# Scores of two units made in one run of matmuls, for six pairs of units

## Chip, cores, metric

The kernel runs on one core of one Trainium2 chip. The metric is the device time of one execution in microseconds (us), lower is better. TensorE is called PE below, VectorE DVE, ScalarE ACT, GpSimd POOL, SyncE SP, as the profile does.

## What is computed

```python
for t in range(S):                       # attention with a decaying state, per batch b and head h
    kt, vt, rt = (k[:, :, t], v[:, :, t], r[:, :, t])
    cur = np.einsum('bhd,bhe->bhde', u[None] * kt, vt)
    y[:, :, t] = np.einsum('bhd,bhde->bhe', rt, state + cur)
    state = w[None, :, :, None] * state + np.einsum('bhd,bhe->bhde', kt, vt)
...
h = np.maximum(xt @ w_tok1, 0.0) @ w_tok2        # mixing over the 768 tokens
u = x + h.transpose(0, 2, 1)
h2 = np.maximum(u @ w_ch1, 0.0) @ w_ch2          # MLP over the channels, 384 to 1536 to 384
return (u + h2).astype(np.float32)
```

There are 4 batches, 8 heads, 768 tokens and 48 channels a head; `x` is `y` with its heads side by side, 768 x 384 a batch.

## The kernel before

**Units.** The recurrence is cut into chunks of 128 tokens. One chunk of one batch with all eight heads is a unit: six units a batch, 24 in all, numbered through. The decay is folded into the operands: `kp` and `rp` multiply a unit's k and r by powers of w. PE transposes the two (`trk`, `trr`), and ACT copies them to SBUF as `rk`; for units 14 to 23 a transposing DMA, `t`, which SP issues, does both. Then come the scores, step `at`: for each of four pairs of heads two matmuls of `k` against `r` that contract 48 rows each, one in partitions 0 to 47 and one in partitions 64 to 111, eight in a unit. They write two PSUM banks, one for each half, `at_ps0` and `at_ps1`. Two steps `AT0` and `AT1` on DVE multiply a bank by the causal mask and write bf16; for the halves named in `raw`, ACT copies first and DVE masks the copy. `y` multiplies the masked scores with v, `yS` adds what the state gives, `kv` and `S` advance the state, and `x` adds the diagonal term `yd` and writes the batch's `x_b`.

**The MLP of a batch** follows when its six units are done: `hid` and `hr` (up over the tokens, relu), `bk` and `us` (down, residual), a turn of the result (`tu` and `uT` on PE and ACT or DVE, or a DMA), `z` (up over the channels: 24 steps of 3 matmuls a batch), `zr` (relu, on ACT or DVE), `h` (down: 6 chunks of 4 steps of 3 matmuls) and `os` (residual), then the store. A step `z1_0_9` is batch 1, tokens' half 0, column block 9; `h1_2_3` is batch 1, chunk 2, fourth quarter. The MLP of one batch runs among the units of the next.

**PSUM.** PSUM has eight banks. Four lie in `psA` (L602): one each for `at_ps0`, `at_ps1`, `y_ps` and `kv_ps`. The other four are the pool `psM` (L603), tag `m`: every `trk`, `hid`, `bk`, `tu`, `z` and `h` takes one of these when PE comes to it and gives it back when the last step that reads it is done (`rk`, `hr`, `us`, `uT`, `zr`, `os`). An `h` chunk keeps its bank through all four quarters.

**What sets the order.** `graph` (L181) makes the steps, what each waits for, which take and give a bank. `ORDER` (L508) is a written list for each of the five engines, and the engine works through its list strictly: where a step must wait, all that stands behind it on that engine waits too. `Plan.run` (L70) merges the five lists into one order in which the instructions are recorded; `fill` (L142, L1052) puts small matmuls on idle data, which nothing reads, into waits of PE before the first `z`.

**What the change touches.** The entry for `at` in `graph` (L276 to L303) with the bank lists after it, the configuration `CFG` (L444), all five lists in `ORDER`, and the function `at` (L821).

Of the kernel before, what the change touches and what calls it, by code (L numbers as in the profile page):

```python
# [12 lines left out]
f32 = mybir.dt.float32  # L13
# [8 lines left out]
B, H, S, D = 4, 8, 768, 48  # L22
T = 128
C = S // T
G = C // 2
HP = H // 2
# [154 lines left out]
def graph(do, cfg):  # L181
# [48 lines left out]
    kus, rkus, adgs, raws, masked = [], [], [], [], []  # L230
    for u in range(NU):
# [44 lines left out]
        at = p.add(f"at{u}", [("PE", t_at * f, t_at * f + 0.2)], [rk, rkk] + at_free, rank=r, emit=do("at", u))  # L276
# [7 lines left out]
        if u in cfg.get("raw2", ()):  # L284
            raw0 = p.add(f"raw0_{u}", [("ACT", 0.5, 0.65)], [atq[0]] + raws[-1:] + masked[-3:][:len(masked) // 3 and 1], rank=r, emit=do("raw", u, 0))
            a0 = p.add(f"AT0_{u}", [("DVE", 0.33, 0.48, True)], [raw0], rank=r, emit=do("ATr", u, 0))
            raws.append(raw0)
            masked.append(a0)
        else:
            raw0 = a0 = p.add(f"AT0_{u}", [("DVE", 0.597, 0.75)], [atq[0]], rank=r, emit=do("AT", u, 0))  # L290
        if u in cfg.get("raw", ()):
            raw = p.add(f"raw{u}", [("ACT", 0.5, 0.65)], [at] + raws[-1:] + masked[-3:][:len(masked) // 3 and 1], rank=r, emit=do("raw", u, 1))
# [3 lines left out]
            at_free = [raw0, raw]  # L296
        else:
            a1 = p.add(f"AT1_{u}", [("DVE", 0.597, 0.75)], [atq[1]], rank=r, emit=do("AT", u, 1))
            at_free = [raw0, a1]
# [138 lines left out]
    for s in p.steps:  # L438
# [60 lines left out]
    y_m=(2, 4),  # L499
    apart=2.0,  # L500
# [70 lines left out]
def kernel(  # L571
# [477 lines left out]
    def do(kind, *args):  # L1049
        return lambda eng: STEPS[kind](eng, *args)  # L1050
# [52 lines left out]
```

## Time and profile before

| | us |
|---|---|
| time, median of 3 executions | 165.9 (165.4 to 166.22) |
| the profiled execution, its own time | 164.99 |
| its span, first to last instruction | 163.2 |

The span and what lies around it differ by 1.79 us. In the profile, almost every instruction carries line L617, since one helper records them all; so groups are told apart by the names of what they write and read: `z_ps` is written by `z`, `h_ps` by `h` and also by `hid` (then it reads `x_b`), `hT_ps` by `bk`, `t_ps` by `tu`, `tr_ps` by `trk` and `trr`, `at_ps` by `at` (and, in three steps ahead of the first `z`, by the turn of batch 0), `kv_ps<-UW,pr` by `pg`, a small product for the diagonal term. A row of a timeline gives the start, the time to the end of the last instruction in the row, and how many instructions it holds. The end of a matmul is modelled and overlaps the next one, so what a matmul costs PE is read from start to start.

### The profile page before, as it was taken

The numbers are of one execution on the slowest core, as the hardware profiler recorded it, in microseconds if no ns is written. First come the engines' busy times: TensorE is split into PE (matmuls) and PEld (weight loads), VectorE is DVE, ScalarE is ACT, GpSimd is POOL, SyncE is SP. The second block draws the span as 40 slices with busy tenths as digits, with TensorE's granted clock in tenths as the row PEclk, the third lists the DMA queues.
The fourth block names the chain that finished last, engine by engine and source line by source line (L and its number), as shares of the span: only waits on it lengthen the run. The fifth ranks groups of instructions, "written<-read, shape, count | busy, mean of one in ns | idle before, by whom it ended". The sixth has DMA issues, their size and how long they took to land.

```text
span 163.2 us, 3866 instructions
## 1 busy us (share of the span) xinstructions
PE 154.2 (95%) x1510; PEld 99.8 (61%) x1510; DVE 115.9 (71%) x245; ACT 73.6 (45%) x158; POOL 69.1 (42%) x85
## 2 busy tenths in 40 slices
PE   6977999999999999899999999999999999999991
PEld 3555876666666667576566665665666666665571
DVE  5369996826397999795969979898989574222621
ACT  4898683362579633656623540082226102731200
POOL 7449860000363977998439201887527100000000
PEclk9999999999999999999999999999999999999999
DMA  5999999999998999889969989999971036100412
GB/s 107 219 218 221 167 185 205 185 184 202 204 220 167 234 237 196 156 143 210 190 153 214 207 203 179 191 220 171 228 184 51 0 72 156 65 0 0 145 54 96
DMA packets 97428, 26.28 MB, mean 161 GB/s; under 512 B 90753, under 2 KB 97410, under 8 KB 97410
## 3 DMA queue, kind: packets, MB, share of 16 engines
q1 hardware_dynamic: 93920, 22.88, 69.0%
q0 software_dynamic: 3488, 3.15, 12.3%
q8 instruction: 12, 0.20, 0.5%
q14 instruction: 6, 0.05, 0.1%
q10 hardware_dynamic: 2, 0.00, 0.0%
HBM read 20.65 MB, written 4.72 MB: 155 GB/s over the span
## 4 chain that ended last, share of the span: by engine, by line
PE 86%; ACT 5%; DVE 5%; issue 2%
PE h_ps L617 33%; PE z_ps L617 27%; PE y_ps L617 5%; PE at_ps L617 5%; PE hT_ps L617 4%; PE tr_ps L617 4%; ACT rk L617 3%; PE kv_ps L617 3%; PE idle_ps L617 2%; DVE AT L617 2%; PE w_ps L617 1%; PE t_ps L617 1%; PE fill_ps L617 1%; DVE pr L617 1%; DVE x_b L617 1%
## 5 line engine op out<-in xcount | busy, mean ns | idle before, releaser
L617 PE MATMUL h_ps<-wch,zr 128*128 128x384 bf16 (+1 forms) x300 | 55.2, 320 | 0.0
L617 ACT ACTIVATE zr<-z_ps 128x384 bf16<-128x384 f32 x66 | 31.1, 492 | 50.0 <-PE z_ps L617 49.8
L617 PE MATMUL z_ps<-uT,wch 128*128 128x384 bf16 x288 | 53.2, 326 | 0.0
L617 PEld LDWEIGHTS <-wch 128*128 128x128 bf16 x288 | 26.9, 98 | 16.2
L617 PEld LDWEIGHTS <-zr 128*128 128x128 bf16 x300 | 27.4, 98 | 14.9
L617 DVE TENSOR_TENSOR AT<-at_ps,mask 128x512 bf16<-128x512 f32 x43 | 28.8, 683 | 1.7 <-PE at_ps L617 1.6
L617 POOL TENSOR_TENSOR kpr<-ld_k,wn 128x384 bf16<-128x384 f32 x18 | 17.8, 996 | 22.2 <-DMA ld_k<-in_k_dram 20.5
L617 DVE TENSOR_SCALAR zr<-z_ps 128x384 bf16<-128x384 f32 x30 | 16.1, 552 | 11.8 <-PE z_ps L617 11.8
L617 POOL TENSOR_TENSOR yd<-vb,adg 128x384 f32<-128x384 bf16 x15 | 12.6, 840 | 21.3 <-DVE adg L617 14.9
L617 ACT COPY rk<-tr_ps 128x512 bf16<-128x512 bf16 (+1 forms) x23 | 15.3, 682 | 12.3 <-PE tr_ps L617 12.2
L617 DVE TENSOR_TENSOR osb<-u_sb,h_ps 128x384 f32<-128x384 bf16 (+1 forms) x22 | 11.7, 533 | 12.0 <-PE h_ps L617 11.8
L617 POOL TENSOR_TENSOR kpr<-ld_r,wp 128x384 bf16<-128x384 f32 x16 | 16.9, 1059 | 7.9 <-DVE x_b L617 2.5
L617 PEld LDWEIGHTS <-kpr 128*128 128x128 bf16 x192 | 12.4, 99 | 6.8 <-issue 2.6
L617 PEld LDWEIGHTS <-rk 48*128 48x128 bf16 (+1 forms) x272 | 10.6, 95 | 7.6 <-issue 3.9
L617 ACT CAST vb<-ld_v 128x384 bf16<-128x384 f32 x24 | 12.1, 513 | 4.1 <-DMA ld_v<-in_v_dram 4.0
L617 DVE TENSOR_TENSOR x_b<-y_ps,yd 128x384 bf16<-128x384 f32 x23 | 12.7, 552 | 0.7 <-PE y_ps L617 0.4
L617 DVE TENSOR_TENSOR u_sb<-x_b,hT_ps 128x384 bf16<-128x384 bf16 x21 | 10.8, 550 | 3.1 <-PE hT_ps L617 3.0
L617 PE MATMUL tr_ps<-ident,kpr 128*128 128x128 bf16 x112 | 10.6, 227 | 2.1 <-ACT rk L617 1.4
L617 PEld LDWEIGHTS <-wtok 128*128 128x128 bf16 x90 | 8.2, 97 | 4.5
L617 PE MATMUL h_ps<-x_b,wtok 128*128 128x384 bf16 x48 | 10.1, 326 | 0.0
L617 PE MATMUL at_ps<-rk 48*128 48x128 bf16 x192 | 9.5, 219 | 0.5 <-ACT rk L617 0.4
L617 POOL TENSOR_TENSOR ku<-ld_k,u_bc 128x384 f32<-128x384 f32 x9 | 8.9, 994 | 0.6 <-DVE kpr L617 0.6
(87 smaller groups left out, 156.4 us busy)
## 6 DMA issues: line engine op xcount, KB each, us to landing
ld_r<-in_r_dram SPq DMA_DIRECT2D x24, 192.0 KB, 3.8
ld_k<-in_k_dram SPq DMA_DIRECT2D x24, 192.0 KB, 3.8
ld_v<-in_v_dram SPq DMA_DIRECT2D x24, 192.0 KB, 3.9
out_dram<-osb SPq DMA_DIRECT2D x23, 192.0 KB, 3.0
wch<-in_moe_w_ch_dram POOLq DMA_DIRECT2D x4, 576.0 KB, 11.8
wtok<-in_moe_w_tok_dram POOLq DMA_DIRECT2D x2, 384.0 KB, 6.3
u_bc<-in_u_dram SPq DMA_DIRECT2D x1, 192.0 KB, 5.4
out_dram<-osb SPq DMA_DIRECT2D x2, 96.0 KB, 1.6
```

Source lines behind the costliest of these rows:

```text
L617: ins = tc.keep_in_program_order(f(*args, **kw))
```

## The change

In six pairs of units (6 and 7, 12 and 13, 14 and 15, 16 and 17, 18 and 19, 22 and 23) the step `at` of the second unit goes, and the first one's makes the scores of both: sixteen matmuls in a row. The first unit's scores go to `at_ps0` and `at_ps1` of `psA` as before. The second unit's go to two banks of `psM`, which two new steps without instructions (`at14_bank0`, `at14_bank1`) reserve; each is given back when the step that reads it (`AT`, or `raw` where ACT copies) is done. The run now waits for the transposed operands of both units.

```diff
+        pairs, give = cfg.get("pairs", ()), [[], []]
+        if u - 1 in pairs:
+            for s in [at] + at_bank:
+                p.wait(s, [rk, rkk])
+            give = [[f"at{u - 1}_bank{q}"] for q in range(2)]
+        elif u in pairs:
+            at_bank = [p.add(f"at{u}_bank{q}", [("PE", 0.0, 0.0)], [rk, rkk] + at_free, take=True, rank=r) for q in range(2)]
+            at = p.add(f"at{u}", [("PE", t_at + 0.14, t_at + 0.29)], [rk, rkk] + at_bank + at_free, rank=r, emit=do("at", u, True))
+        else:
+            at = p.add(f"at{u}", [("PE", t_at * f, t_at * f + 0.2)], [rk, rkk] + at_free, rank=r, emit=do("at", u))
...
-            at_free = [raw0, a1]
+            free = [raw0, a1]
+        if u - 1 not in pairs:
+            at_free = free
...
+    pairs=(6, 12, 14, 16, 18, 22),
...
-    def at(eng, i):
+    def at(eng, i, both=False):
...
+        if both:
+            L[i + 1]["at"] = [psM.tile([128, HP, T], f32, name=f"at_ps{q}", tag="m") for q in range(2)]
+        for n in range(i, i + 1 + both):
+            L[n]["AT"] = [None, None]
+            for a in range(HP):
+                for q in range(2):
+                    half = slice(q * P, q * P + D)
+                    pe.matmul(L[n]["at"][q][:, a, :], L[n]["rk"][half, 0, a, :], L[n]["rk"][half, 1, a, :],
+                              start=True, stop=True)
```

All five lists of `ORDER` are written anew as well, from the first step to the last. PE's step list holds the same work but for the pairs; eight more `zr`, one more `uT` and one more `os` stand on DVE instead of ACT, five `adg` more on ACT instead of DVE; SP issues the same 112 transfers in another order; PE's program has 44 fill matmuls instead of 50. Its list around units 14 and 15, a line of each:

```diff
-        "z1_0_0 z1_0_5 z1_0_9 z1_0_8 tu1_5 z1_0_1 tu1_4 z1_0_6 z1_0_11 z1_1_0 at14 z1_0_10 z1_1_3 z1_0_4 z1_0_2 z1_0_7 y13 z1_0_3 at15 "
+        "z1_1_6 z1_1_3 z1_0_3 z1_1_1 y13 z1_1_2 kv14 z1_0_6 z1_0_11 h1_1_0 yS14 at14_bank0 h1_1_1 at14_bank1 at14 h1_0_0 h1_0_1 h1_1_2 "
```

Three places show what moved. First PE, at the last matmuls of unit 14's scores. Before, `rk_1471` is unit 14's operand, `at_ps0_1587` and `at_ps1_1588` its two banks, and the `z` of the MLP follows at once:

```order
L617 LDWEIGHTS rk_1471
L617 MATMUL at_ps0_1587<-rk_1471 128x128
L617 LDWEIGHTS rk_1471
L617 MATMUL at_ps1_1588<-rk_1471 128x128
L617 LDWEIGHTS wch1_154
L617 MATMUL z_ps_1600<-uT_1264,wch1_154 128x384
```

Now unit 14's last two (`rk_1583`) are followed by the first of unit 15 (`rk_1522`), which write two banks of `psM`, `at_ps0_1682` and `at_ps1_1683`:

```order
L629 LDWEIGHTS rk_1583
L629 MATMUL at_ps0_1680<-rk_1583 128x128
L629 LDWEIGHTS rk_1583
L629 MATMUL at_ps1_1681<-rk_1583 128x128
L629 LDWEIGHTS rk_1522
L629 MATMUL at_ps0_1682<-rk_1522 128x128
L629 LDWEIGHTS rk_1522
L629 MATMUL at_ps1_1683<-rk_1522 128x128
```

Between the two units' scores there is no other matmul now, where six `z` and one `y` stood between `at14` and `at15` before. Behind the run stand `h1_0_0 h1_0_1 h1_1_2 h1_1_3 z1_1_9 kv15 y14`.

Second, DVE at the masks of these two units. Before, unit 14's two `AT` stand together, and unit 15's come with other work between:

```order
L617 TENSOR_TENSOR AT1_1616<-at_ps1_1588,mask_114 128x512
L617 TENSOR_TENSOR AT0_1622<-at_ps0_1587,mask_114 128x512
L617 TENSOR_TENSOR S0_1631<-kv_ps_1329,bm_137 128x384
L617 TENSOR_SCALAR zr_1510<-z_ps_1612 128x384
L617 TENSOR_TENSOR x_b2_158<-y_ps_1465,yd_1578 128x384
L617 TENSOR_REDUCE adg_1665<-rku_1533 128x8
L617 TENSOR_TENSOR AT1_1677<-at_ps1_1648,mask_114 128x512
```

Now all four stand within six rows, and unit 15's first bank is read ahead of unit 14's second:

```order
L629 TENSOR_TENSOR AT0_1704<-at_ps0_1680,mask_114 128x512
L629 TENSOR_TENSOR AT0_1713<-at_ps0_1682,mask_114 128x512
L629 TENSOR_REDUCE adg_1613<-rku_1458 128x8
L629 TENSOR_TENSOR AT1_1727<-at_ps1_1681,mask_114 128x512
L629 TENSOR_SCALAR zr_1586<-z_ps_1632 128x384
L629 TENSOR_TENSOR AT1_1759<-at_ps1_1683,mask_114 128x512
```

Third, DVE at the start of the program, where no pair stands. Before, unit 0 goes ahead: `kp0`, `rp0`, then `kp1` (`kpr0_123` holds unit 0's products, `kpr1_125` unit 1's):

```order
L617 TENSOR_TENSOR kpr0_123<-ld_k_162,wn_146 128x8x48
L617 TENSOR_TENSOR kpr0_123<-ld_r_160,wp_147 128x8x48
L617 TENSOR_TENSOR kpr1_125<-ld_k_168,wn_146 128x8x48
L617 TENSOR_TENSOR AT0_230<-at_ps0_210,mask_114 128x512
L617 TENSOR_TENSOR pr_240<-tr_ps_185,rk_198 128x512
```

Now unit 1's k product stands between unit 0's two, and the diagonal's `pr` ahead of the mask:

```order
L629 TENSOR_TENSOR kpr0_123<-ld_k_162,wn_146 128x8x48
L629 TENSOR_TENSOR kpr1_125<-ld_k_160,wn_146 128x8x48
L629 TENSOR_TENSOR kpr0_123<-ld_r_164,wp_147 128x8x48
L629 COPY wu_sb_148<-wu_ps_211 128x4
L629 TENSOR_TENSOR UW_133<-wu_sb_148,wu_ps_211 64x4 x2
L629 TENSOR_TENSOR pr_244<-tr_ps_188,rk_202 128x512
L629 TENSOR_TENSOR AT0_251<-at_ps0_234,mask_114 128x512
```

Unit 0's r product moved one place back, and on ACT the table for unit 1's k (`wn1`) now stands ahead of unit 0's (`wn0`).

More of the change, by code (lines that the diff above doesn't have):

```diff
@@ L284, in graph @@
         if u in cfg.get("raw2", ()):
-            raw0 = p.add(f"raw0_{u}", [("ACT", 0.5, 0.65)], [atq[0]] + raws[-1:] + masked[-3:][:len(masked) // 3 and 1], rank=r, emit=do("raw", u, 0))
+            raw0 = p.add(f"raw0_{u}", [("ACT", 0.5, 0.65)], [atq[0]] + raws[-1:] + masked[-3:][:len(masked) // 3 and 1], rank=r, give=give[0], emit=do("raw", u, 0))
             a0 = p.add(f"AT0_{u}", [("DVE", 0.33, 0.48, True)], [raw0], rank=r, emit=do("ATr", u, 0))
@@ L289, in graph @@
         else:
-            raw0 = a0 = p.add(f"AT0_{u}", [("DVE", 0.597, 0.75)], [atq[0]], rank=r, emit=do("AT", u, 0))
+            raw0 = a0 = p.add(f"AT0_{u}", [("DVE", 0.597, 0.75)], [atq[0]], rank=r, give=give[0], emit=do("AT", u, 0))
         if u in cfg.get("raw", ()):
-            raw = p.add(f"raw{u}", [("ACT", 0.5, 0.65)], [at] + raws[-1:] + masked[-3:][:len(masked) // 3 and 1], rank=r, emit=do("raw", u, 1))
+            raw = p.add(f"raw{u}", [("ACT", 0.5, 0.65)], [at] + raws[-1:] + masked[-3:][:len(masked) // 3 and 1], rank=r, give=give[1], emit=do("raw", u, 1))
             a1 = p.add(f"AT1_{u}", [("DVE", 0.33, 0.48, True)], [raw], rank=r, emit=do("ATr", u, 1))
@@ L295, in graph @@
             masked.append(a1)
-            at_free = [raw0, raw]
+            free = [raw0, raw]
         else:
-            a1 = p.add(f"AT1_{u}", [("DVE", 0.597, 0.75)], [atq[1]], rank=r, emit=do("AT", u, 1))
-            at_free = [raw0, a1]
+            a1 = p.add(f"AT1_{u}", [("DVE", 0.597, 0.75)], [atq[1]], rank=r, give=give[1], emit=do("AT", u, 1))
+            free = [raw0, a1]
+        if u - 1 not in pairs:
+            at_free = free
         if cfg.get("at_one"):
@@ L826, in at @@
             L[i]["at"] = [psA.tile([128, HP, T], f32, name=f"at_ps{q}", tag=f"at{q}") for q in range(2)]
-        L[i]["AT"] = [None, None]
-        for a in range(HP):
-            for q in range(2):
-                half = slice(q * P, q * P + D)
-                pe.matmul(L[i]["at"][q][:, a, :], L[i]["rk"][half, 0, a, :], L[i]["rk"][half, 1, a, :],
-                          start=True, stop=True)
+        if both:
[7 more added lines that the diff above has]
+                              start=True, stop=True)
     def AT(eng, i, q):
```

1 line of the change is left out of this document (removed), and 92 rows, old and new, of the table ORDER.

## Prediction

> **What bounds the kernel now.** I read the page first, for which engine carries the end, then the busy time by stage, then who PE waits for.
>
> ```profile
> span 163.2 us, 3866 instructions
> PE 86%; ACT 5%; DVE 5%; issue 2%
> ```
>
> The chain that ends last runs over PE for 86% of the span. The stages tell where the other 14% lie (busy us of each engine in a stretch, its count of instructions in brackets; then the granted clock and the DMA engines' share):
>
> ```profile
> core 0: us, PE busy (x) PEld busy (x) DVE busy (x) ACT busy (x) POOL busy (x), PEclk, DMA share, GB/s
> 0.00:28.50 28.50, 24.38 (x307) 17.14 (x308) 21.19 (x56) 20.40 (x43) 16.97 (x30) 1.00 1.05 189
> 28.50:42.00 13.50, 13.50 (x99) 8.57 (x97) 8.02 (x16) 4.98 (x12) 0.00 (x0) 1.00 1.18 191
> 42.00:68.00 26.00, 24.57 (x331) 16.72 (x328) 21.40 (x46) 16.50 (x33) 18.11 (x20) 1.00 0.99 204
> 68.00:80.00 12.00, 12.00 (x119) 7.54 (x117) 9.63 (x21) 7.47 (x18) 9.95 (x11) 1.00 0.99 180
> 80.00:96.00 16.00, 16.00 (x159) 10.19 (x157) 14.04 (x28) 6.05 (x14) 6.74 (x7) 1.00 0.91 193
> ...
> 136.00:159.80 23.80, 23.80 (x159) 14.90 (x156) 8.18 (x16) 6.70 (x15) 0.00 (x0) 1.00 0.24 72
> ```
>
> Three parts. Up to 28.5 us, where the first `z` begins, PE has gaps. From 42 to 68 us, where units 6 to 13 run among the MLP of batch 0, it misses 26.00 - 24.57 = 1.43 us. Elsewhere from 28.5 us to its last matmul it misses nothing, at the full clock. So past 68 us each microsecond that PE does not have to spend is worth a microsecond, and each that it is made to wait costs one. What PE waited for from 28.5 to 160 us is all here (who, total us, times, longest):
>
> ```profile
> PE tr_ps L617 <- ACT rk L617: 0.9, 3, 0.5
> PE kv_ps L617 <- DVE S L617: 0.6, 2, 0.4
> ```
>
> **What a run of scores costs.** These rows are of unit 14's `at`, from timelines cut off at later and later moments, so that the count in the row grows:
>
> ```profile
> 75.18 0.65 PE L617 MATMUL z_ps<-uT,wch 128*128 128x384 bf16 x3
> 75.76 0.23 PE L617 MATMUL at_ps<-rk 48*128 48x128 bf16 x2
> ...
> 75.76 0.40 PE L617 MATMUL at_ps<-rk 48*128 48x128 bf16 x8
> 76.09 0.34 PE L617 MATMUL z_ps<-uT,wch 128*128 128x384 bf16 x1
> ```
>
> The pace of `z` matmuls comes from a long run of the chain, and all later runs of scores have one row in the groups from 28.6 us on:
>
> ```profile
> 136.86 7.31 PE z_ps L617 x45
> L617 PE MATMUL at_ps<-rk 48*128 48x128 bf16 x144 | 7.2, 219 | 0.0
> ```
>
> One `z` matmul takes 7.31 / 45 = 0.162 us. The three `z` that start at 75.18 are through at 75.18 + 3 x 0.162 = 75.67; the scores begin at 75.76, 0.09 later. Six more matmuls after the first two lengthen the row from 0.23 to 0.40, so two of them, one in each half of the rows, take 0.17 / 3 = 0.057 us together, and four twos 0.23. They would be through at 75.99; the next `z` starts at 76.09, 0.10 later. **A run of eight costs PE 76.09 - 75.67 = 0.42 us: 0.23 of work and 0.19 of going in and coming out.** The 144 matmuls are 18 runs of 7.2 / 18 = 0.40 us, the same as the row above, so this holds for all of them. It also holds at any neighbour with 128 rows, and no other product from `kv0` on contracts fewer than 128 rows.
>
> **What the pairs save.** Six times two runs become one of sixteen: 2 x 0.42 = 0.84 us becomes 0.42 + 0.23 = 0.65, 0.19 less a pair, **1.14 us in all**. No trace shows a run of sixteen. Inside a run of eight the matmuls change half at every step at 0.057 us for two, and the second unit's are of the same shape; what remains is that unit's waits on its operand and its banks, which may hold the run up in the middle. So the saving lies between 0 and 1.14; I take 1.14, as the row of a run's inside is the nearest. Pair 6 runs in the stretch where PE waits now and then; if its share is lost in such a wait, 0.95 is left.
>
> **What the two banks cost.** The second unit's scores hold two of the four banks that `z`, `h`, `bk`, `tu` and `trk` take in turn, from the run's start until DVE (or ACT) has read them. The price of a mask, and of what stands between, from the page and from one packed stretch of DVE:
>
> ```profile
> L617 DVE TENSOR_TENSOR AT<-at_ps,mask 128x512 bf16<-128x512 f32 x43 | 28.8, 683 | 1.7 <-PE at_ps L617 1.6
> L617 ACT ACTIVATE zr<-z_ps 128x384 bf16<-128x384 f32 x66 | 31.1, 492 | 50.0 <-PE z_ps L617 49.8
> 83.01 0.56 DVE L617 TENSOR_TENSOR S<-kv_ps,wGm 128x384 bf16<-128x384 f32 x1 [1.55 <-PE kv_ps L617]
> ...
> 83.95 0.68 DVE L617 TENSOR_TENSOR AT<-at_ps,mask 128x512 bf16<-128x512 f32 x1
> 84.55 0.55 DVE L617 TENSOR_SCALAR zr<-z_ps 128x384 bf16<-128x384 f32 x1
> 85.01 0.55 DVE L617 TENSOR_TENSOR x_b<-y_ps,yd 128x384 bf16<-128x384 f32 x1
> 84.80 0.34 PE kv_ps L617 x5
> ```
>
> A mask keeps DVE 84.55 - 83.95 = 0.60 us from start to start (0.68 to its end), a `zr` 0.46. Take pair 14 and count from the moment at which PE goes on behind the run. The masks can begin some 0.1 later, when the last scores are out (the run's row ends at 75.76 + 0.40 = 76.16, its successor starts at 76.09). By DVE's new rows unit 15's first bank is read at 0.1 + 0.60 + 0.68 = 1.4, `AT1_14` is done at 0.1 + 2 x 0.60 + 0.47 (the `adg`, taken as a step of the usual length) + 0.68 = 2.45, the second bank at 2.45 + 0.46 + 0.60 = 3.5. On PE, `h1_0_0` takes the last bank; then come three steps that take none, so `z1_1_9` asks for one after 4 x 3 x 0.162 = 1.95, 0.55 after the first is free; `y14` asks for `AT1_14` after 1.95 + 0.49 + 0.34 (`kv15`, the last row above) = 2.78, 0.33 after it is there. So I cost the banks at **nothing**: what hides them is the `h` steps behind each run. If that cover goes, because DVE comes to the run more than 0.33 us late, PE waits the excess at each pair, and with it all that stands in its list. From below nothing: a wait of PE cannot be shorter than none, so no gain is in it. From above: one unit's two masks, 2 x 0.60 = 1.2 us, at each of six pairs, 7.2 us.
>
> Behind DVE's four masks in a row stand `S`, `x` and `os` of the same units, 2 x 0.60 later than behind two; in DVE's new list fewer other steps stand between them, the work is the same.
>
> The Trainium skill has a rule against this change: "TensorEngine Tiling (Array Packing)", under Gotcha 1: PSUM Pressure, says that row tiling raises the pressure on PSUM, as different row tiles need different banks, and its PSUM Bottleneck part that tiling speeds up TensorE but not the emptying of PSUM. Here that would be four masks of DVE against one run of PE, and by it the sum below would be up to 7.2 us dearer; the trace of before, where the scores have two banks of their own and no wait past 68 us names them, does not show it, and four banks at once are in no run yet.
>
> **What the new lists cost.** All five are new, so two places can move without any pair.
>
> ```profile
> 0.00:5.00 5.00, 3.69 (x9) 1.71 (x10) 2.27 (x15) 2.59 (x5) 4.00 (x16) 1.00 0.66 130
> 5.00:11.00 6.00, 4.88 (x48) 3.29 (x46) 3.03 (x8) 5.40 (x12) 2.95 (x4) 1.00 1.09 216
> 11.00:25.80 14.80, 13.10 (x232) 10.46 (x232) 14.59 (x29) 10.95 (x25) 10.02 (x11) 1.00 1.14 195
> 4.36 0.61 ACT L617 ACTIVATE wn<-lnw,iota 128x384 f32<-128x384 f32 x1
> 4.88 1.10 ACT L617 ACTIVATE wp<-lnw,iota 128x384 f32<-128x384 f32 x2
> wch<-in_moe_w_ch_dram POOLq DMA_DIRECT2D x1, 576.0 KB, 7.8
> 19.86 0.77 POOL L617 DMA_DIRECT2D wch<-in_moe_w_ch_dram  x1
> 28.51 1.79 PE L617 MATMUL z_ps<-uT,wch 128*128 128x384 bf16 x10
> ```
>
> *The front, up to 28.5 us.* From 11 to 25.8 us DVE is busy 14.59 of 14.80: its work there is what sets when batch 0's last `x` is done, and the new list holds the same steps. Before that it idles half the time (3.03 of 6.00). There unit 0 is now served later: `wn0` behind `wn1` is 4.88 - 4.36 = 0.52 us, `rp0` behind `kp1` another step of 0.47, so up to 1.0 us dearer if all of it reaches the end; unit 1 is served earlier by about as much, which DVE's later idle time can take. From the other side, the first `z` needs the first half of `wch`, which lands at 19.86 + 7.8 = 27.66, and its load stands as far back in POOL's list as before: not more than 28.51 - 27.66 = 0.85 can be won. Bounds -0.85 to +1.0; I take 0, since the row nearest to it is the packed one.
>
> *From 42 to 68 us.* PE's 1.43 us of waits hang on `rk` and `S` of units 6 to 13, in lists that are new. They can all go (-1.43) or come twice (+1.43), as each has a step's length of cover and not more; taken as 0. Eight more `zr` on DVE are 8 x 0.46 = 3.7 us; by the lists three lie in batch 0, three in batch 1, three fewer in batch 2 and five in the last stage, where DVE is busy 8.18 of 23.80. I cost them at nothing; the cover is DVE's idle time.
>
> **The sum** against the profiled execution: 164.99 - 1.14 + 0 + 0 + 0 = 163.85. The median of the runs shown, 165.9, lies 0.91 above that execution, so **164.8** for a median. The measurement of this kernel can tell about 0.5%, 0.83 us, from no change: below 165.07 is faster, above 166.73 slower.
>
> **The rivals.**
> - *Banks run out (slower).* DVE is the second tightest engine: 14.04 of 16.00 us in the stretch with units 14 to 17, and packed from 83 us on. If it comes to a pair's masks late by 0.33 + w, PE waits w. From w = 0.19 the pairs bring nothing; from (1.14 + 0.83) / 6 = 0.33 the kernel is slower. With w = 0.5, DVE one ordinary step and a half late, it is 164.8 + 6 x 0.5 = 167.8. For it: the missing slack in DVE. Against it: before, DVE was as full, and PE waited for none of its steps past 68 us. Chance 0.14. The Trainium skill's rule on PSUM pressure, "TensorEngine Tiling (Array Packing)", Gotcha 1, would be right in this case.
> - *The lists give the gain back (same).* The front takes half of its dear end, 0.5, and the waits from 42 to 68 us grow by about 0.3: 164.8 + 0.8 = 165.6. For it: both are stretches in which waits, not PE's work, set the pace. Against it: nothing in them takes more work than before. Chance 0.22.
> - *The pair is no pair (same).* PE stops within the run for the second unit's operand or banks and pays the 0.19 after all: 165.9. For it: the second unit's operand comes by its own transfer. Against it: these stand several steps ahead in SP's and PE's lists. Chance 0.06.
> - *The new lists also win.* The front comes near the landing of `wch` (-0.85) and half of the 1.43 goes: 164.8 - 0.85 - 0.7 = 163.2. For it: six fewer fills, which stand only where PE waits in the front. Chance 0.08.
>
> **How the numbers follow.** The forecast, 164.8, has a chance of 0.50, and with the last rival faster has 0.58; the second and third make 0.28 for within 0.5%; the first makes slower 0.14. The range, 163.4 to 166.4, leaves out the slow case and most of the best one, and holds the front's bounds on the forecast (163.9 to 165.8).
>
> **What would show it.** Right: a run of sixteen scores in a row of about 0.40 + 0.23 = 0.63 us, no PE wait at the `z` or `y` behind it, PE busy throughout from about 68 us on, and the first `z` within 0.5 us of 28.5. Wrong: rows of `z_ps`, `h_ps` or `y_ps` that wait for DVE `AT`, for DVE `zr` or for ACT `zr` behind a pair (banks); gaps inside the sixteen (no pair); a first `z` past 29 us or more than 2 us of PE idle from 42 to 68 us (lists).

## The result, and the profile after

| | before | changed |
|---|---|---|
| median of the executions, us | 165.88 | 169.24 (167.59, 167.6, 170.87, 171.69) |
| ratio, with its 95% interval | | 1.0106 [1.0063, 1.0149] |
| profiled execution, us | 164.99 | 167.60 |
| its span, us | 163.2 | 165.6 |

The changed kernel is about 1% slower; forecast was 164.8 us. Two of its four executions took more than 1.5% longer than its fastest and are left out of the ratio, as such executions are in all ratios below; the profiles of e2 and e8 are of such ones.

The page, the same two lines as shown of before, and between them the granted clock in 40 slices of the span:

```profile
span 165.6 us, 3841 instructions
...
PEclk9999699999999999999999999999999999999998
...
PE 81%; SPq 6%; DMA 5%; ACT 3%; DVE 1%; issue 1%; POOL 1%; DVEq 0%
```

PE's share of the chain fell from 86% to 81%; SP's queue of loads and the DMAs now hold 11% of it. The fifth slice, 16.6 to 20.7 us, ran at 0.6 of the clock. The stages, in the columns that the prediction explains:

```profile
0.00:28.50 28.50, 23.30 (x290) 16.17 (x290) 20.94 (x54) 19.55 (x40) 16.79 (x30) 0.94 0.99 177
...
42.00:68.00 26.00, 24.82 (x314) 17.15 (x313) 20.89 (x44) 14.93 (x32) 15.59 (x17) 1.00 1.04 218
...
80.00:96.00 16.00, 16.00 (x169) 10.29 (x168) 14.90 (x30) 6.23 (x14) 12.34 (x14) 1.00 1.20 213
...
136.00:159.80 23.80, 23.80 (x153) 14.62 (x151) 11.34 (x22) 4.79 (x10) 0.00 (x0) 1.00 0.25 75
```

Up to 28.5 us PE is busy 23.30 us against 24.38, at a mean clock of 0.94; from 80 us on it misses nothing. Three dates split the span's growth of 2.37 us. The first `z` starts at 30.61 (its row is below) instead of 28.51: **+2.10**. From there to the end of the last matmul it takes 130.59 (161.20 - 30.61) instead of 131.29: **-0.70**. From the last matmul to the end of the span it takes 165.56 - 161.20 = 4.36 instead of 163.19 - 159.80 = 3.39: **+0.97**.

```profile
30.61 0.65 PE L629 MATMUL z_ps<-uT,wch 128*128 128x384 bf16 x3
```

**The pairs** work as they were meant to. The run of units 14 and 15, and the row of all scores past 30 us:

```profile
83.96 0.62 PE L629 MATMUL at_ps<-rk 48*128 48x128 bf16 x16
84.51 1.80 PE L629 MATMUL h_ps<-wch,zr 128*128 128x384 bf16 x10
```

```profile
L629 PE MATMUL at_ps<-rk 48*128 48x128 bf16 x144 | 6.1, 218 | 0.0
```

Sixteen take 0.62 (forecast 0.63) without a gap, and the 144 matmuls keep PE 6.1 us, where it was 7.2. Past 75 us the list of PE's waits is empty: no bank is named there.

**The front.** POOL's and PE's rows around unit 4's second operand, and one of the fills behind it:

```profile
16.66 1.00 POOL L629 TENSOR_TENSOR kpr<-ld_r,wp 128x384 bf16<-128x384 f32 x1 [2.99 <-DMA ld_r<-in_r_dram]
17.59 0.89 POOL L629 DMA_DIRECT2D wtok<-in_moe_w_tok_dram  x1
```

```profile
17.71 0.47 PE L629 MATMUL tr_ps<-ident,kpr 128*128 128x128 bf16 x4 [1.90 <-POOL kpr L629]
...
19.39 1.05 PE L629 MATMUL fill_ps<-idle 128*128 128x128 bf16 x8
```

POOL's `rp4` waits 2.99 us for the load `r4`, PE's `trr4` waits 1.90 for `rp4`, and POOL's next step, the first weight load `w0` (384 KB), is issued at 17.59 instead of 15.67. Behind the wait PE runs at half its clock from 17.9 to 21.3 us: 8 fills take 1.05 us (0.61 at the full clock, in e10's trace). In the 3.6 us before that PE was busy for 1.51 us:

```profile
14.30:17.90 3.60, 1.51 (x31) 1.35 (x31) 2.91 (x7) 2.69 (x7) 1.24 (x2) 1.00 0.68 134
```

The Trainium skill, "TensorE: Matmul & The Clock Gate", Part 1: The HAM clock gate, has TensorE fall to half its clock after an idle window of about 3.4 us. The length of the slow stretch, 3.41 us, agrees with that window; but PE was not idle for all of it here, it was busy 1.51 of 3.60 us, and its clock fell all the same.

When `r4` landed, by the row of its issue (size, us from issue to landing), in the changed kernel and in the one before:

```profile
ld_r<-in_r_dram SPq DMA_DIRECT2D x1, 192.0 KB, 5.7
```

```profile
ld_r<-in_r_dram SPq DMA_DIRECT2D x1, 192.0 KB, 3.6
```

It was issued at nearly the same time (10.86, before 10.99) and took 2.1 us longer. The front was not late until then: `at0`, the scores of unit 0, starts at 8.90 (before 8.22), but `at2` at 13.18 (before 14.31).

**The tail.** DVE's last `os`, and in the chain the store that it waits for; then the same steps before:

```profile
158.28 0.55 DVE L629 TENSOR_TENSOR osb<-u_sb,h_ps 128x384 f32<-128x384 bf16 x1 [0.42 <-PE h_ps L629]
...
162.22 0.35 DVE L629 TENSOR_TENSOR osb<-u_sb,h_ps 128x192 f32<-128x192 bf16 x1 [1.37 <-DMA out_dram<-osb]
```

```profile
158.87 3.23 DMA out_dram<-osb
```

```profile
156.88 0.56 DVE L617 TENSOR_TENSOR osb<-u_sb,h_ps 128x384 f32<-128x384 bf16 x1 [2.92 <-PE h_ps L617]
...
159.84 0.35 DVE L617 TENSOR_TENSOR osb<-u_sb,h_ps 128x192 f32<-128x192 bf16 x1 [0.39 <-PE h_ps L617]
```

`osb` has three buffers, so `os3_5b` needs the one of `os3_3` back. In both kernels `os3_3` starts 2.92 us before the last matmul is done (161.20 - 158.28, 159.80 - 156.88), yet now its store is 1.02 us too late. Two transfers, then, `r4` and this store, were slow for no reason that the lists show.

### The profile page after: what moved, and what is told of

Its sections match the earlier page's. It is cut to its first block, busy times and chain, and to the rows that moved or that the text cites. A ratio compares the mean times of both kernels' runs of the same rounds, so it can differ in the third digit from the quotient of the medians.

```text
span 165.6 us, 3841 instructions
## 1 busy us (share of the span) xinstructions
PE 154.3 (93%) x1504; PEld 100.5 (61%) x1504; DVE 120.2 (73%) x248; ACT 70.1 (42%) x152; POOL 71.2 (43%) x88
## 4 chain that ended last, share of the span: by engine, by line
PE 81%; SPq 6%; DMA 5%; ACT 3%; DVE 1%; issue 1%; POOL 1%; DVEq 0%
PE h_ps L629 31%; PE z_ps L629 28%; SPq L629 6%; PE at_ps L629 5%; PE y_ps L629 4%; PE hT_ps L629 4%; DMA ld_r<-in_r_dram 3%; PE tr_ps L629 3%; PE kv_ps L629 3%; DMA out_dram<-osb 2%; ACT rk L629 1%; PE t_ps L629 1%; PE fill_ps L629 1%; POOL kpr L629 1%; DVE osb L629 1%
## 5 line engine op out<-in xcount | busy, mean ns | idle before, releaser
L629 ACT ACTIVATE zr<-z_ps 128x384 bf16<-128x384 f32 x58 | 27.6, 493 | 51.9 <-PE z_ps L629 51.8
L629 PEld LDWEIGHTS <-wch 128*128 128x128 bf16 x288 | 26.7, 98 | 15.8
L629 DVE TENSOR_TENSOR AT<-at_ps,mask 128x512 bf16<-128x512 f32 x43 | 28.1, 683 | 2.8 <-PE at_ps L629 2.7
L629 POOL TENSOR_TENSOR kpr<-ld_k,wn 128x384 bf16<-128x384 f32 x18 | 18.0, 1004 | 26.6 <-DVE pr L629 21.3
L629 DVE TENSOR_SCALAR zr<-z_ps 128x384 bf16<-128x384 f32 x38 | 20.5, 555 | 9.9 <-PE z_ps L629 9.3
L629 POOL TENSOR_TENSOR kpr<-ld_r,wp 128x384 bf16<-128x384 f32 x16 | 16.5, 1038 | 8.4 <-DMA ld_r<-in_r_dram 5.7
L629 POOL TENSOR_TENSOR yd<-vb,adg 128x384 f32<-128x384 bf16 x16 | 13.3, 829 | 14.2 <-DVE adg L629 7.4
L629 PEld LDWEIGHTS <-rk 48*128 48x128 bf16 (+1 forms) x272 | 11.1, 97 | 6.9 <-issue 3.7
L629 POOL TENSOR_TENSOR ku<-ld_k,u_bc 128x384 f32<-128x384 f32 x10 | 10.2, 1022 | 7.7 <-DVE x_b L629 3.8
L629 PE MATMUL hT_ps<-h1r,wtok 128*128 128x384 bf16 x42 | 9.4, 326 | 0.1
```

Source lines behind the costliest of these rows:

```text
L629: ins = tc.keep_in_program_order(f(*args, **kw))
```

## The experiments

First z, then first z to the last matmul, then how far the last `os` starts behind the last matmul, of each run's profile, and the ratio to the kernel before on the same chip:

| run | first z | z to end | os | ratio |
|---|---|---|---|---|
| before | 28.51 | 131.29 | 0.04 | |
| changed | 30.61 | 130.59 | 1.02 | 1.011 [1.006, 1.015] |
| e1_old_front | 29.44 | 131.78 | 0.04 | 1.002 [0.997, 1.006] |
| e2_new_front | 34.14 | 132.12 | 0.35 | 1.015 [1.002, 1.029] |
| e3_r4_first | 43.52 | 131.40 | 0.03 | 1.077 [1.065, 1.089] |
| e4_last_store | 31.84 | 130.66 | 0.04 | 1.002 [0.997, 1.007] |
| e5_after_again | 28.94 | 130.58 | 1.15 | 1.006 [1.002, 1.010] |
| e6_split_run | 33.29 | 132.56 | 0.33 | 1.033 [1.030, 1.037] |
| e7_twelve_rows | 29.89 | 131.06 | 0.35 | 1.011 [1.004, 1.018] |
| e8_old_loads | 33.27 | 131.59 | 0.04 | 1.011 [1.005, 1.017] |
| e9_w0_behind | 30.03 | 131.52 | 0.32 | 1.012 [1.008, 1.016] |
| e10_w0_early | 33.71 | 131.29 | 0.04 | 1.019 [1.015, 1.023] |
| e11_old_front_store | 30.45 | 131.78 | 0.04 | 1.013 [1.010, 1.016] |
| e12_mended | 30.50 | 131.05 | 0.03 | 1.008 [1.005, 1.011] |
| e13_rp5_first | 32.79 | 131.79 | 0.03 | 1.012 [1.000, 1.024] |
| e14_kp5_first | 29.32 | 132.60 | 0.42 | 1.004 [0.998, 1.009] |
| e15_late_seam | 29.15 | 131.88 | 0.04 | 0.999 [0.994, 1.003] |
| e16_fetch_earlier | 31.29 | 131.56 | 0.04 | 1.004 [0.999, 1.009] |
| e17_before_fetch | 30.94 | 131.29 | 0.04 | 0.997 [0.992, 1.001] |

Chips and executions differ: e5 is the changed kernel itself on another chip, with its first z at 28.94. So one profile's front is one draw; what stands below of the front goes by which load landed when.

### Which part loses

**e1 and e2** put the lists of one kernel up to the first `z` ahead of those of the other behind it; e1 has the pairs, e2 has none. The first line of PE's list in e1:

```diff
-        "trk0 trk1 trr0 wu at0 trk2 pg0 trr1 trk3 y0 kv0 at1 trr2 trr3 pg1 at2 yS1 trk4 y1 kv1 trr4 at3 pg3 yS2 kv2 at4 trk5 pg2 trr5 kv3 "
+        "trk0 trr0 wu at0 trk1 trr1 trk2 kv0 pg0 at1 trk3 y0 pg1 trr2 yS1 kv1 at2 trr3 y1 kv2 pg2 trk4 at3 trr4 yS2 y2 yS3 trk5 trr5 "
```

> The changed kernel, with the lists of before up to the first z (all five engines, units 0 to 5) and the new lists behind it, pairs and all. Front theory (the 2.1 us are lost before the first z, the pairs save their 1.1 us): first z near 28.5 us, span near 165.6 - 2.1 = 163.5, time near 165.5, and below 165.0 if the last store is not held up as well. Rival, bank theory (the loss is in the stretch with pairs): first z near 28.5 us too, but the time stays above 166.7, with PE waits past 68 us.

> The kernel before, without pairs, with the new lists up to the first z and its own behind it. Front theory: first z near 30.6 us, time near 165.9 + 2.1 = 168.0. Bank theory: the front costs little by itself, time within 0.8 us of 165.9.

e1's time is not told apart from that of the kernel before; e2, with no pair in it, loses 1.5% (by three executions; 0.2 to 2.9%). That speaks for the new front and against the pairs as the place of the loss. It is not the whole of it: e11 below, which has e1's lists, comes out at 1.013. And e1 gains nothing: ten more fills stand right ahead of its first `z` (28.63 to 29.44), where old lists meet new ones, and its first z's are another 0.6 us apart from each other for work that stands between them. In e2 PE waits somewhere else than in the changed kernel:

```profile
PE kv_ps L618 <- ACT vb L618: 3.0, 1, 3.0
```

`kv3` waits 3.0 us for `vb3`, whose load `v3` landed 6.85 us behind its issue, 4.0 before. So the new front has two ways to lose.

**e3** issues `r4` ahead of `r5` on SP; **e8** has SP's loads in the old order.

```diff
-i:r5 i:r4 i:v2 i:k5 i:v5 i:v3 i:v4
+i:r4 i:r5 i:v2 i:k5 i:v5 i:v3 i:v4
```

```diff
...
-i:v1 i:r5 i:r4 i:v2 i:k5 i:v5 i:v3 i:v4
+i:v2 i:r4 i:v4 i:r5 i:k5 i:v3 i:v5
```

> The changed kernel with two loads swapped in SP's list, r4 ahead of r5. Load theory (the front is late because r4 lands at 16.6 us, where PE and POOL wait for it): r4 lands about 0.9 us earlier or more, PE's wait before trr4 shrinks from 1.9 us to under 0.9, the first z comes at 28.7 to 29.7, time 165.6 to 166.6. Rival, list theory (unit 0's later start and the order of the masks set the front): first z stays within 0.4 us of 30.6.

> The changed kernel with the 18 loads of units 0 to 5 in the order of before in SP's list, all else new. Load theory (v4 as the last load and r4 behind r5 make unit 4 late): PE's waits before trr4 and kv3 or kv4 fall from over 2.5 us together to under 1, first z at 28.5 to 29.3. Rival (POOL's and ACT's lists set the front): first z not before 30.

e3 tells little of the time: the planner put 185 fills ahead of `kv4`, where they cost PE 10 us. But `r4` landed at 14.16 and `at3` started 1.5 us earlier (16.67), so the wait for `r4` was gone; then `kv3` waited 2.9 us. e8 missed the same way: `r4` on time, `kv3` late.

```profile
PE kv_ps L630 <- ACT vb L630: 2.1, 1, 2.1
```

In both, POOL was free early and issued `w0` at 15.2 and 15.8 us, beside SP's `v3`. That gave the theory of the **race**: `w0` and a v load that is still on its way go through the DMA engines together, and the v load comes late.

**e4** gives the last `os` buffers of their own (tiles of the v loads, which are over by then).

```diff
+        if parts > 1:
+            M[b]["o", c, part] = lpool.tile([128, dm], f32, name="ld_v")[:, 0:dm // parts]
+        else:
```

> The changed kernel, in which the two halves of the last output chunk get buffers of the load pool, so that os3_5b need not wait until an earlier store has left its buffer. Store theory (os3_5b waited 1.4 us for the store of o3_3, which took 3.2 us): os3_5b starts within 0.3 us of the last matmul's end, span 1.0 us shorter, time near 166.6. Rival (the end is late for PE alone): no change, 167.6.

```profile
161.79 0.35 DVE L629 TENSOR_TENSOR ld_v<-u_sb,h_ps 128x192 f32<-128x192 bf16 x1 [0.43 <-PE h_ps L629]
162.54 0.35 DVE L629 TENSOR_TENSOR ld_v<-u_sb,h_ps 128x192 f32<-128x192 bf16 x1 [0.39 <-PE h_ps L629]
```

The last `os` follows its matmuls at once (162.54, last matmul 162.50). This is the 1.0 us of the tail. The ratio with it is 1.002; the profiled execution is no shorter than that of the changed kernel (span 166.1), as its first `z` came at 31.84.

**e5** is the changed kernel once more, **e6** separates the two units of a run by one matmul of 128 rows, **e7** puts 6 small matmuls (12 rows of PE's program) ahead of the first.

```diff
+            if n > i:
+                pe.matmul(L[n]["at"][0][:, 0, :], idle[:, 0:128], idle[:, 0:128], start=True, stop=True)
```

```diff
+    for _ in range(6):
+        pe.matmul(idle_ps[:, 0:8], idle[:, 0:128], idle[:, 0:8], start=True, stop=True)
```

> The changed kernel as it is, beside the next three on one chip. Front theory (before the first z it hangs on loads): from its first z to its last matmul 130.6 us again, within 0.3, while the first z moves between 29 and 33 us. Rival (the loss is fixed in the lists): first z at 30.6 within 0.3.

> The changed kernel with one matmul of idle data, 128 rows by 128 columns, between the two units' scores in each pair; the scores overwrite what it writes. Pair theory (what a pair saves is one going in and coming out of the 64-row form, 0.19 us): each pair costs 0.19 + 0.06 more, the stretch from the first z to the last matmul 6 x 0.25 = 1.5 us more than in the changed kernel, 132.1. Rival (the saving lies in the new lists): 6 x 0.06 more, 131.0.

> The changed kernel with six matmuls of 8 columns on idle data more among the first ones, which lengthen PE's program by the twelve rows that it is shorter than before. Fetch theory (PE's instructions are fetched 16 KB at a time, each fetch tied to a row of its program, and the last one stood before the store of o3_3): every fetch comes earlier by about twelve rows, the last one about 1 to 2.5 us earlier against the last matmul, and os3_5b no longer waits, 1.0 us less at the end. Rival (the end's wait comes from the order of the last h steps alone): os3_5b waits about 1 us again.

The split run of units 14 and 15 in e6:

```profile
75.67 0.40 PE L629 MATMUL at_ps<-rk 48*128 48x128 bf16 x8
76.00 0.23 PE L629 MATMUL at_ps<-idle 128*128 128x128 bf16 x1
76.16 0.40 PE L629 MATMUL at_ps<-rk 48*128 48x128 bf16 x8
76.49 0.34 PE L629 MATMUL z_ps<-uT,wch 128*128 128x384 bf16 x1
```

It keeps PE 76.49 - 75.67 = 0.82 us, the whole one 84.51 - 83.96 = 0.55. Of the 0.27 the added matmul is 0.056 (the pace of such rows), so **a pair saves 0.21**. Six times 0.27 are 1.62 of the 1.97 us that e6 takes more than the changed kernel from its first `z` to its last matmul (132.56, 130.59); most of the rest is a wait of `z` for a turn by DMA (0.3). e6's slower time has its front in it as well (first z 33.29): there `r4` took 4.0 us, and `v3` 6.6. e7 moved PE's program against its own ends, and the wait of the last `os` went from 1.02 to 0.35: the slow store depends on the place of something in PE's program.

e5 and e7 also give a price for the fall of the clock. In both `r4` landed at nearly the same time (15.81 and 15.90). From 16.9 to 20.3 us the granted clock was 1.00 in e5 and 0.50 in e7, and the first `z` came at 28.94 and 29.89: an estimate of 0.9 us for one such fall, from these two executions. With `r4` late by this much and no fall, e5's first `z` is only 0.43 us behind that of before.

### Why loads come late

That something is in the list of DMA queues: a queue of kind "instruction", 12 packets a run, each of 16 KB, where PE has 1504 matmuls and as many weight loads. The first of them in the changed kernel, in a stretch of 0.2 us from 14.4 us on (packets, MB, share of 16 engines):

```profile
q8 instruction: 1, 0.02, 32.0%
```

0.32 x 16 x 0.2 = 1.02 us of one DMA engine, starting at 14.53, when `r4` was the next load to land (3.6 us behind its issue would have been 14.5). Before, it comes at 15.42, when `r4` has landed. The Trainium skill, "DMA: Bandwidth & Descriptors", Queues, rings and completion order, says that a DMA engine takes its queues in turn, a whole packet at a time. By that rule a packet that lasts 1 us holds up a load that is spread over all 16, and these rows agree. **e16** and **e17** move the fetch: 50 small matmuls ahead in the changed kernel, 30 in the one before.

```diff
+    for _ in range(50):
+        pe.matmul(idle_ps[:, 0:8], idle[:, 0:128], idle[:, 0:8], start=True, stop=True)
```

> The changed kernel with 50 small matmuls on idle data (100 rows of PE's program) ahead of the first real one, in PE's empty time before 5.4 us; all else as in the changed kernel. Theory (the load that is next to land when PE's first instruction fetch moves its 16 KB comes 1 to 2 us late; in the changed kernel that is r4, in the one before it is not): the first fetch moves from 14.5 to between 10 and 12 us, r4 lands by 15.2 instead of 16.6, PE's wait for unit 4's second transposes shrinks from 2.1 to under 1 us, and a load that is next to land behind the fetch (r3, k4 or v1) takes 4.6 us or more from issue to landing instead of 3.6 to 4.0. Its first z and its time may be no better, as that load, and w0 issued earlier beside v3 and v4, can cost as much. Rival (r4 is late because of its place in SP's list): r4 lands past 15.7 as before, 4.8 us or more behind its issue.

> The kernel before with 30 such matmuls (60 rows) ahead of its first real one. Theory: the first fetch moves from 15.4 to between 12.5 and 14.2 us, while r4 (issued at 11.0) is the next to land; r4 then takes 4.6 us or more and lands past 15.4 instead of 14.55, rp4 and w0 on POOL move back by about 1 us, and the first z comes at 29 to 30.5 us instead of 28.5, the time at 166.4 to 168. If the fetch falls below 12.4 us it is k4 or v2 that is late, and r4 is not. Rival (the fetch does not hold loads up): every load lands within 0.3 us of where it lands in the kernel before, first z within 0.3 us of 28.5.

e16's fetch came at 12.0 us. The load that was next to land then, `v1`, and the fetch (0.603 x 16 x 0.1 = 0.96 us):

```profile
ld_v<-in_v_dram SPq DMA_DIRECT2D x1, 192.0 KB, 4.9
...
q8 instruction: 1, 0.02, 60.3%
```

`k4`, which landed at 12.23, took 4.0; `v1` took 4.9, `r5` behind it 4.7, `r4` 4.4 instead of 5.7, and no wait of PE for POOL's `rp4` was left. That is the theory's pattern; its number for `r4` (by 15.2) was missed, it landed at 15.76, where the rival had it (past 15.7), though not with the rival's 4.8 us or more. The time did not come down to that of before: `w0` went out at 16.77, 0.3 us ahead of `v4`, which then took 7.0, and the 50 matmuls were not free, PE's first transposes start at 7.43 instead of 6.04. In e17 the fetch moved less than expected, to 14.69; `r4` landed 0.5 us behind its start and was on time, and `v4`, the next, took the blow:

```profile
ld_r<-in_r_dram SPq DMA_DIRECT2D x1, 192.0 KB, 3.6
...
ld_v<-in_v_dram SPq DMA_DIRECT2D x1, 192.0 KB, 4.8
```

Both runs thus say that moving the fetch moves the delay from one load to another (`v1` 4.9 for 3.9, `v4` 4.8 for 3.9). Over all traces, loads that landed up to 1.05 us behind the start of the first fetch took 3.6 to 4.1 us, and the next one to land behind these took 4.5 to 5.7 (17 traces; in the other two the landing is not on record, or `w0` is beside it). It is not always the load next to land: in e2 and e6, with SP's list of the changed kernel, `r4` landed 0.5 and 0.8 us behind the start and took 4.0, and `v2` behind it paid. What decides whether `r4` is hit stays open. e17's time is not told apart from that of before (0.997 [0.992, 1.001]), but its profiled execution has its first `z` at 30.94, with `v3` late by the race below and PE's first transposes at 6.91 instead of 6.00 for the 30 matmuls.

**The last store** is late for the same reason. In the changed kernel the last fetch starts at 159.37, 0.5 us behind the issue of `os3_3`'s store; in e16 it is at 155.18, long over when that store goes out at 160.52. The fetch in the changed kernel, in the 0.2 us from 159.3 on, and the store in e16:

```profile
q8 instruction: 1, 0.02, 42.4%
...
out_dram<-osb SPq DMA_DIRECT2D x1, 192.0 KB, 1.9
```

The store took 3.23 us in the changed kernel and 1.85 in e16, where the last `os` waits no more (0.04 in the table) with the buffers as they were. In the 14 traces without e4's buffers the last `os` is 0.32 to 1.16 us behind where the last fetch starts 1.8 to 2.9 us ahead of the last matmul's end, and 0.04 where it starts 3.1 us ahead or more.

**The race** has its own pair: **e9** moves `w0` behind `kp5` in the changed kernel, **e10** ahead of `kp4` in the one before.

```diff
-rp1 kp2 kp3 rp3 kp4 rp4 i:w0 kp5 rp5 i:w1
+rp1 kp2 kp3 rp3 kp4 rp4 kp5 i:w0 rp5 i:w1
```

```diff
-rp1 kp2 kp3 rp3 kp4 rp4 i:w0 rp5 kp5 i:w1
+rp1 kp2 kp3 rp3 i:w0 kp4 rp4 rp5 kp5 i:w1
```

> The changed kernel with one step moved: POOL issues the weight load w0 (384 KB) behind kp5 instead of ahead of it, so behind the loads v3 and v4 of SP whatever POOL waits for. Theory of the race (w0 ahead of v3 and v4 holds these up, and kv3 with them): w0 issued at 18 us or later, v3 landed by 20.5 and v4 by 22 us, no wait of PE above 0.5 us at the kv of unit 3; the wait of PE for POOL's rp4 (r4 landing late) may stay at 1.4 to 2.1 us; first z between 29 and 31 us, median 166.5 to 168 and no execution of 170 us. Rival (the times of 170 us have nothing to do with the loads): single executions of 170 us or more as in the changed kernel, and v3 landing as there.

> The kernel before with one step moved: POOL issues w0 ahead of kp4 instead of behind rp4, at about 13.6 us and so ahead of SP's v3 (14.6 us). Theory of the race: v3 lands after 21.5 us instead of 18.6, PE waits 1.5 to 3 us at the kv of unit 3, the first z is at 31 to 33.5 us instead of 28.5, and the time is 168.5 to 171. Rival (only POOL's kp4 and rp4, which stand behind the issue, come later): v3 still lands before 20 us, first z at 28.5 to 29.4 us, time 165.9 to 166.8.

The loads of `v3` in e9, then in e10:

```profile
ld_v<-in_v_dram SPq DMA_DIRECT2D x1, 192.0 KB, 3.7
```

```profile
ld_v<-in_v_dram SPq DMA_DIRECT2D x1, 192.0 KB, 6.9
```

e9 came as the race has it: no wait at `kv3`, no execution above 168.07, median 167.5. It does not decide, though: `v3` took 3.8 in the changed kernel's profile too, and these are four executions. The first half of `wch`, behind `w0` on the same queue, landed at 29.99 and held the first z's up by 1.0 us. e10 does: with `w0` alone moved, `v3` took 6.9 us instead of 4.0 and landed at 21.04, near what was expected. The 5 us to the first `z` are not its doing alone, and the wait expected at `kv3` is not among PE's: `k5` was late as well, 22 fills in one place ran at half the clock, and a mask of DVE took 2.98 us beside POOL (last section). Over all traces: where `w0` is issued 0.44 us or less behind `v3`, or ahead of it, `v3` takes 6.5 to 6.9 us (e2, e3, e6, e8, e10, e17); where it is 1.07 to 2.6 us behind, 3.5 to 5.5 (before, changed, e1, e4, e5, e7, e9, e14, e15, e16), with one exception, e11, 6.7 at 1.27 us. There `r5`, ahead of it, had taken 4.9 us behind the fetch; that this is why, was only argued.

### What is left when these are mended

**e11** is e1 with the last stores of e4. **e12** takes e9's order on POOL, e4's stores, and on SP `r4` ahead of `r5` and `v5` last. **e13** is e12 with `rp5` first on POOL, **e14** the kernel before with `kp5` ahead of `rp5`.

```diff
-i:r5 i:r4 i:v2 i:k5 i:v5 i:v3 i:v4
+i:r4 i:r5 i:v2 i:k5 i:v3 i:v4 i:v5
```

```diff
-rp4 kp5 i:w0 rp5 i:w1
+rp4 rp5 i:w0 kp5 i:w1
```

```diff
-rp4 i:w0 rp5 kp5 i:w1
+rp4 i:w0 kp5 rp5 i:w1
```

> The old lists up to the first z, the new ones with the pairs behind it, and the last stores from buffers of their own, so that the last residual waits for no store. If the loss of the changed kernel is all in the front and in the last store, this keeps the pairs' gain: first z 28.5 to 29.4 us, first z to last matmul 130.3 to 131.8 us, the last residual within 0.1 us of the last matmul, time 164.8 to 165.9. Rival (the new lists behind the first z lose by themselves what the pairs save): first z to last matmul as before, 131.3 us or more, and time 165.9 or more.

> The changed kernel with three amends: w0 behind kp5 on POOL, on SP r4 ahead of r5 and v3, v4 ahead of v5, and the last stores from buffers of their own. If the loss is r4's late landing, the race of w0 with v3 and v4, and the last store, nothing of it is left: PE waits under 0.7 us for unit 4's transposes, under 0.3 us at the kv of unit 3, first z at 27.8 to 29.2 us, the last residual right behind the last matmul, time 164.2 to 165.4, faster than both kernels. Rival (the new lists of DVE, ACT and PE in the front are slower by themselves): first z past 29.5 us with the loads on time, time above 166.

> The mended kernel (loads and last stores amended) with POOL's front in another order: rp5, then w0, then kp5, where the mended one has kp5, w0, rp5. Theory: the new list lets rp5, whose load is there at 14.9 us, wait behind kp5, whose load lands at 17.5, so that unit 5's second transposes and all weight loads come about 1 us late. Then here rp5 ends by 16.5 us instead of 20.5, trr5 starts by 20 us, w1 is issued by 18.9 instead of 20.4, the first half of wch lands by 29.2 instead of 30.5, the first z is at 28.8 to 29.8 us and the time 0.5 to 1.2 us below that of the mended kernel. Against it the race of w0 with v4: if v4 lands past 21.5 us, PE waits up to 0.7 us more at the kv of unit 4. Rival (the lists of DVE, ACT and PE set the front's end): first z still past 30 us and the time within 0.4 us of the mended kernel's.

> The kernel before with two steps of POOL exchanged, kp5 ahead of rp5, as in the changed one. Theory (this exchange delays unit 5): kp5 still waits for its load until 18.2 us, rp5 ends at 20 instead of 17.6 us, trr5 starts 0.6 to 1.0 us later than 20.14, the four transfers behind it are issued about 0.9 us later, first z at 29.0 to 29.6 us instead of 28.5 and the time 166.1 to 167. Rival: PE has slack there, first z within 0.25 us of 28.5 and the time within 0.4 us of the one before.

e11 missed: the race hit `v3` even in the old front, and the ten fills at the seam took 0.8 us ahead of the first `z`. It has e1's lists and, within 0.1 us, e1's median (167.57 and 167.55); the ratios differ because the kernel before ran at a median of 167.9 beside e1 and of 165.7 beside e11. e12 missed too, and the rival's numbers came. Loads and tail were in order, and its first z still late:

```profile
PE z_ps L630 <- DMA wch<-in_moe_w_ch_dram: 1.0, 2, 0.6
PE tr_ps L630 <- POOL kpr L630: 0.8, 1, 0.8
```

`w0` behind `kp5` goes out at 18.60, and the half of `wch` that the first `z` needs lands at 30.45. In every trace but that of e10 it lands 11.6 to 13.4 us behind `w0`'s issue (15.67 to 27.64 before, 17.59 to 29.55 in the changed kernel, 18.60 to 30.45 here). So `w0` late puts the first `z` late, and `w0` early puts the v loads late. The other wait is `rp5`, which sits behind `kp5` in the new list, while `k5` is the later load. e13, made to undo that, had its fetch on `r5` (`rp5` done at 18.08, not by 16.5), and PE lost 1.9 us elsewhere:

```profile
PE kv_ps L630 <- ACT vb L630: 1.9, 1, 1.9
```

`w0` was 0.6 us behind the last v load, `v5`, which took 4.8 us; ACT's new list has `vb5` ahead of `vb4`, and `kv4` needs `vb4`. e12's own order of loads had set that trap. e14 gives 0.8 us to the first `z` (29.32), as expected, of which 0.6 is a wait for `wch`; `trr5` came 0.23 later and not 0.6, and z to end holds a wait of 1.0 us for a transposing DMA at 97 us. The time is not told apart from before (1.004 [0.998, 1.009]); this exchange costs little by itself.

**e15** keeps all old lists until batch 0's first `z` are through, with the pairs, the new lists behind that, and e4's stores. PE's list changes over at unit 6:

```diff
-h0_0_2 h0_0_3 trk6 trr6 h0_2_1 h0_1_2 trk7 h0_1_3 trr7 z0_1_9 kv6 pg6 h0_2_2 at6_bank0 at6_bank1 at6
+h0_0_2 h0_0_3 trk6 trr6 h0_1_2 trk7 h0_1_3 trr7 z0_1_9 kv6 pg6 at6_bank0 at6_bank1 at6
```

> All five lists as before until batch 0's first z are through (PE up to trk6), from there on the new ones with the six pairs, a few steps of the new lists moved where the old and the new meet, and the last stores from buffers of their own. The first z must be that of before, 28.2 to 28.9 us. If what the change itself does is a gain of 0.2 us a pair, and all the loss lies in the lists ahead of the first z and in the last store: first z to last matmul 130.0 to 130.8 us (131.3 before), the last residual within 0.1 us behind, and the time 164.3 to 165.4, below both kernels. Rival (the waits that the new lists bring from 42 to 75 us eat the pairs up): first z to last matmul 131.2 us or more and the time within 0.4 us of before or above it.

```profile
PE tr_ps L630 <- ACT rk L630: 1.5, 3, 0.8
PE z_ps L630 <- DMA uT<-u_sb: 0.3, 1, 0.3
```

It is the best run with pairs, 0.999 [0.994, 1.003] (its median is 166.6 us), and not the gain forecast: the rival's number came. From the first `z` to the last matmul it takes 131.88 us against 131.29. PE's busy time from 42 to 75 us, in e15, then changed, then before:

```profile
42.00:75.00 33.00, 31.07 (x385) 21.30 (x383) 27.67 (x58) 19.64 (x43) 21.52 (x23) 1.00 0.95 194
```

```profile
42.00:75.00 33.00, 31.34 (x386) 21.48 (x385) 26.92 (x56) 18.98 (x41) 21.55 (x23) 1.00 0.96 200
```

```profile
42.00:75.00 33.00, 31.57 (x400) 21.39 (x397) 27.82 (x60) 21.12 (x44) 24.21 (x26) 1.00 0.98 194
```

PE misses 33.00 - 31.07 = 1.93 us from 42 to 75 us, against 1.43 before and 1.66 in the changed kernel; 0.4 go at 141 us, where `z` waits for a turn by DMA. The remaining 0.9 us or so between these and the pairs' 1.26 are spread over many starts; which steps they belong to stays open. No version beat the kernel before.

## Why the prediction was wrong

- **What a run costs, what a pair saves**: right. 0.19 was forecast, 0.21 measured (e6), 1.26 for six; the row of all scores fell by 7.2 - 6.1 = 1.1. The rivals "the pair is no pair" and "the new lists also win" did not come.
- **The banks at nothing**: right. No wait of PE is named past 75 us in the changed kernel, and the slower rival, banks that run out, did not come about. The Trainium skill's rule on PSUM pressure, "TensorEngine Tiling (Array Packing)", Gotcha 1, did not show here.
- **42 to 68 us at nothing, ±1.43**: within its bounds. By windows PE misses 26.00 - 24.82 = 1.18 us there against 1.43, and 0.48 us from 68 to 80, where it missed nothing; to 75 us it is 1.66 against 1.43 (all of it stands about 2 us later than before). Of the pairs' 1.26 a net 0.70 is left at the last matmul.
- **"Bounds -0.85 to +1.0; I take 0, since the row nearest to it is the packed one"**: this step failed. The front brought +2.10 in the profile, past its dear end. It was worked out from DVE's steps alone; the dear end priced `wn0` and `rp0`. Unit 0 was indeed 0.68 us late by them (`at0`), but `at2` was 1.13 us ahead again, so neither is what came late. What sets the front is when loads land. The working looked at `wch`'s place in POOL's list, "as far back in POOL's list as before"; but its issue depends on when POOL's `rp4` is done, and that on `r4`. SP's new order, with `v4` 18th instead of 14th, was not priced at all, though the order of transfers was known to be new. The traces show four prices: a load on its way at PE's first fetch, 0.5 to 2.1 us; a v load beside `w0`, 2.5 to 3 us; `wch` 12 us behind `w0`; and a fall of PE's clock behind such a wait, some 0.9 us (e7 against e5, an estimate). The rival "the lists give the gain back" named the place, at 0.5 for the front.
- **The end of the sum**: it stopped at the last matmul. The wait of the last `os` for a store, 1.02 us, is not in it, and no rival had it. e4 and e16 take it away, e7 most of it.
- The sum with the measured terms: 164.99 + 2.10 - 0.70 + 0.97 = 167.36, and 0.24 more around the span gives the profiled 167.60.
- **The signs to look for** were good: "a first `z` past 29 us" names the lists as the cause, and e2, the new front without pairs, has its first `z` at 34.14.

That the fetch delays loads and the last store, and that `w0` delays a v load, is shown by runs that move each alone (e16, e17 and e10). That these delays are the whole of the front's loss is not: with the loads on time, e12's first `z` was still at 30.50, for `w0` and `rp5`. How much of the 1% each has on average is not settled either: the front differs between executions of one kernel (first z 30.61 and 28.94 in two profiles of the changed one).

## What to carry to other kernels

When lists are written anew, price the start by its transfers: for each load, what lies in flight beside it, which engine's wait delays the next issue, and how far the last weight lands behind the first one's issue. A gain of 0.2 us per site on the bounding engine is real but small against one load that lands 2 us late. Follow the sum to the last store and not only to the last matmul.

## What the hardware showed unexpectedly

- PE's own program comes in by DMA during the run: 12 packets of 16 KB, each 0.9 to 1.5 us on one DMA engine in the changed kernel (the first 1.02). A load behind the first one takes 4.5 to 5.7 us instead of 3.6 to 4.1, and a store of 192 KB beside the last one 3.23 instead of 1.85.
- PE busy 1.51 of 3.60 us was little enough for half the clock in the next 3.4 us of the changed kernel.
- A bf16 mask of DVE in e10 beside POOL's weight issue and two of POOL's products, which usually takes 0.4 to 1.1 us:

```profile
13.66 2.98 DVE L618 TENSOR_TENSOR AT<-raw,mask_b 128x512 bf16<-128x512 bf16 x1
```
